# Pooled attention feeding a tanh-shrink MLP: the order of the first loads, and what follows from it

## Chip, cores and metric

The kernel runs on one core of a Trainium2 chip. The time is the device time of one execution in microseconds, as the median of several executions. A profiled execution gives a trace beside it: every instruction of each engine, every DMA, and the clock that was granted to TensorE.

## What is computed

```python
# q, k, v: (8 batches, 8 heads, 576 positions, 64); w_in (512, 2048); w_out (2048, 512)
k_p = k.reshape(B, H, 72, 8, D).mean(axis=3)        # keys and values pooled by 8
v_p = v.reshape(B, H, 72, 8, D).mean(axis=3)
attn = softmax(q @ k_p.T / sqrt(D))
x = (attn @ v_p).transpose(0, 2, 1, 3).reshape(4608, 512)
h = x @ w_in
out = (h - tanh(h)) @ w_out
```

## The kernel before

**Stages.** The 4608 tokens are treated in nine groups of 512 (`g` from 0 to 8): of each batch, the first 512 positions are a group, and the last 64 positions of all eight batches make the ninth. For a group, the hidden layer is computed in 16 tiles of 128 (`mlp_h` for group 0, `h_pair` later): TensorE multiplies by `w1b`, ScalarE takes tanh, VectorE subtracts into `Gt`. Then comes the output product with `w2b`. Group 0 does it plainly (`mlp_o(0, tb, qd, gts)`: token block `tb`, quarter `qd` of the hidden tiles, in the order 0, 8, 4, 12); later groups use a scheme of seven block products with sums of weights (`w2s`) and of tiles, which VectorE prepares (`w_sum`, called as `sum0` to `sum3`) while group 0's output is computed.

**Pooling and layout.** For each batch, 576 pooled rows (8 heads of 72) are loaded as four pairs of heads (144 rows each): 128 rows of each pair as tile `t` from 0 to 3 (`load_main`), and the 16 left-over rows of each pair together as tile `NM` = 4 (`load_dense`, 64 partitions of 2 KB, or `load_left` in four small loads). `pool_k` adds the eight positions in three VectorE steps (lines 268, 276, 281) into `kd`. TensorE turns `kd` by a matmul with the identity (`turn_tile`, L363), and VectorE copies the result into `KB` (`kb_main`, `kb_left`). q is cast (L891), turned on TensorE (`q_pe_transpose`, L228) and copied by ScalarE (L144). `scores_wide` multiplies q by KB (L409) and takes exp on ScalarE (L424). The v of batch 0 is pooled on TensorE (`v_pe_pool`, L900) out of `v_bf`, then masked by VectorE into `VB`. `av_pair` multiplies E by VB (L498) and divides (L954, L955); `x0_turn` turns x for the hidden layer.

**Order.** The whole order is written out by hand[...]. Loads are issued by three engines: SyncE (SP) for k of batch 0, ScalarE for q of batch 0 and for the left-over rows of k and v, GpSimd (POOL) for everything that is cast while it is loaded (v of batch 0, `w1b`, `w2b`, q of batch 1), and for v of batch 1. `after(load_k(1), w1_dmas[1])` makes SP hold back k of batch 1 until w1's second quarter has landed; `after(load_k(2), w2_dmas[2])` likewise holds back k of batch 2 until the third load of w2 has landed. `warm_pe` issues matmuls on zeros, of no use but to keep TensorE busy. [...]

Batch 1's attention runs in among group 0's MLP: `pool_k(1, nc.gpsimd, last=nc.vector)` has GpSimd do the first addition and VectorE the two others, with the reorder of q (`q1_reorder`, L256) between them; then `k_transpose`, `q_pe_transpose`, `scores_wide` stand between the `mlp_o` groups.

Of the kernel before, what the change touches and what calls it, by code (L numbers as in the profile page):

```python
# [8 lines left out]
FP32 = mybir.dt.float32  # L9
# [20 lines left out]
NT = 5  # L30
# [4 lines left out]
NM = 4  # L35
# [8 lines left out]
def kernel(  # L44
# [9 lines left out]
    nc = tc.nc  # L54
# [75 lines left out]
        .rearrange("p (h d) -> p h d", h=H)  # L130
    )
    q_raws = {}
    rot = [0]

    def ps_any(shape, dtype, name):
        pool, tag = [(ps_a, "ps_a"), (ps_h, "hT_ps")][rot[0] % 2]
        rot[0] += 1
        return pool.tile(shape, dtype, name=name, tag=tag)

    evac_n = [0]  # L140

# [7 lines left out]
    def load_main(src, dst, b, t0, t1, eng=nc.sync):  # L149
        return eng.dma_start(out=dst[:, t0:t1, :], in_=src[b, 0:128, t0:t1, :])  # L150
# [7 lines left out]
    def load_dense(src, dst, b, eng=nc.sync):  # L158
        return eng.dma_start(
            out=dst[0 : NM * LO, NM, :], in_=src[b, 128:PR, :, :]  # L160
        )

    def load_k(b, eng=nc.sync):
        return [
            load_main(k_pairs, k_raw[b % 2], b, 0, NM, eng),
            load_dense(k_pairs, k_raw[b % 2], b, eng),
        ]
# [86 lines left out]
    def q1_reorder():  # L254
        for h in (0, 4):
            nc.vector.tensor_copy(  # L256
                out=q_bf[:, 0:R, h : h + 4, :].rearrange("p j h d -> p h j d"),
                in_=q1_bf[:, h : h + 4, :, :],
            )

    def pool_k(b, eng, t0=0, t1=NT, last=None, dep=None):
        r = k_raw[b % 2].rearrange("p t (j d) -> p t j d", d=D)[:, t0:t1, :, :]
        if b not in kdups:
            kdups[b] = work.tile([128, NT, 2, D], BF16, name="kd", tag="kd", bufs=1)
        kd = kdups[b][:, t0:t1, :, :]
        n = t1 - t0
        for ta, tb in halves(n, b):
            first = eng.tensor_tensor(  # L268
                out=r[:, ta:tb, 0:4, :],
                in0=r[:, ta:tb, 0:4, :],  # L270
                in1=r[:, ta:tb, 4:8, :],
                op=ALU.add,
            )
            if dep is not None and ta == 0:
                after([first], dep)
        (last or eng).tensor_tensor(
            out=r[:, :, 0:2, :], in0=r[:, :, 0:2, :], in1=r[:, :, 2:4, :], op=ALU.add
        )
        if b == 1:
            q1_reorder()  # L280
        kd_done = (last or eng).tensor_tensor(
            out=kd,
            in0=r[:, :, 0:1, :].to_broadcast([128, n, 2, D]),
            in1=r[:, :, 1:2, :].to_broadcast([128, n, 2, D]),
            op=ALU.add,
        )
        return kd_done
# [68 lines left out]
    def kb_left(kb, ps, eng):  # L356
        eng(
            out=kb[D:128, :].rearrange("p (t x) -> p t x", x=KP)[:, :, 128 : 128 + LO],
            in_=ps[D:128, 0 : NM * LO].rearrange("p (x t) -> p t x", t=NM),
        )  # L360

    def turn_tile(dst, kd, t):
        nc.tensor.matmul(  # L363
            dst,
            lhsT=kd[:, t, :, :].rearrange("p a d -> p (a d)"),
            rhs=ident[:, :],
            start=True,
            stop=True,
        )
# [47 lines left out]
    def scores_wide(b, ts):  # L417
        if b not in E_tiles:
            E_tiles[b] = work.tile([128, H, S], BF16, name="E", tag="E", bufs=1)[:, 0:NT, :]
        E = E_tiles[b]  # L420
        for t in ts:
            ps = ps_any([128, QA], FP32, "s_ps")
            score_mms(b, t, ps[:, :], False)
            nc.scalar.activation(out=E[:, t, 0:QA], in_=ps[:, :], func=ACT.Exp, scale=SCALE)  # L424
# [350 lines left out]
        .rearrange("p (t n) -> p t n", t=NT)  # L775
    )
    zeros = xT_last[:, 3, :, :].rearrange("p f c -> p (f c)")
    w1_dmas = []
    w2_dmas = []

    def load_w1(c):
        w1_dmas.append(
            nc.gpsimd.dma_start(
                out=w1b[:, :, c * 512 : (c + 1) * 512], in_=w1_src[:, :, c * 512 : (c + 1) * 512]
            )
        )

    def load_w2(i, n):
        w2_dmas.append(
            nc.gpsimd.dma_start(out=w2b[:, i : i + n, :], in_=w2_src[:, i : i + n, :])  # L790
        )

    def after(lds, dep):
        for ld in lds:
            tc.add_manual_dep(
                ld.ins,
                dep.ins.name,
                mybir.DependencyInfo(mybir.DependencyClass.Sync, mybir.DependencyReason.DATA),
            )

    def warm_pe(n, cols=512, b0=4):
        for _ in range(n):
            nc.tensor.matmul(  # L803
                bank(b0, [128, cols]), lhsT=zeros[:, 0:128], rhs=zeros[:, 0:cols], start=True, stop=True
            )
# [3 lines left out]
    def load_q0(h0, h1):  # L809
        return nc.scalar.dma_start(  # L810
            out=t0[:, h0:h1, 0:R, :],
            in_=q[0, h0:h1, 0:QA, :].rearrange("h (p j) d -> p h j d", j=R),
        )
# [5 lines left out]
    load_q0(0, 2)  # L819
    load_main(k_pairs, k_raw[0], 0, 1, 2)  # L820
    load_q0(2, 4)
    load_main(k_pairs, k_raw[0], 0, 2, 4)
    load_q0(4, 8)
    load_dense(k_pairs, k_raw[0], 0, nc.scalar)
    load_dense(v_pairs, v_raw[1], 0, nc.scalar)

    warm_pe(9)
# [28 lines left out]
        out=spread.rearrange("p (t x) -> p t x", x=32)[:, :, 0:LO],  # L856
        in_=ident[:, 0 : NM * LO].rearrange("p (x t) -> p t x", t=NM),
    )
    for c in range(4):
        load_w1(c)  # L860
    load_w2(0, 4)
    nc.gpsimd.tensor_copy(out=v_bf[:, NM, :], in_=v_raw[1][:, NM, :])
    nc.gpsimd.dma_start(out=q1_tail[:QT], in_=q[1, :, QA:S, :].rearrange("h p d -> p h d"))
    nc.gpsimd.dma_start(
        out=q1_bf, in_=q[1, :, 0:QA, :].rearrange("h (p j) d -> p h j d", j=R)
    )
    load_w2(8, 4)
    nc.gpsimd.memset(w2s[64:128, 3, 6:8, :], 0.0)
    nc.gpsimd.memset(k_raw[1][:, NM, :], 0.0)
    nc.gpsimd.memset(v_raw[0][:, NM, :], 0.0)  # L870
    nc.gpsimd.memset(KB[1][:, :], 0.0)
    load_main(v_pairs, v_raw[1], 1, 0, 2, nc.gpsimd)
    load_w2(4, 4)

    after(load_k(1), w1_dmas[1])

    def k_turn(ta, tb):
        ps = ps_any([128, tb - ta, 128], FP32, "kT_ps")
        for t in range(ta, tb):
            turn_tile(ps[:, t - ta, :], kdups[0], t)  # L880
        kb_main(KB[0], ps, ta, tb, (nc.vector.tensor_copy, nc.vector.tensor_copy))

    def k_turn_left():
        ps = ps_any([128, 128], FP32, "kT_ps")
        turn_tile(ps[:, :], kdups[0], NM)
        kb_left(KB[0], ps, nc.vector.tensor_copy)

    pool_k(0, nc.vector, 0, 1)
    pool_k(0, nc.vector, 1, 2)
    def q_turn(eng, h0, h1):  # L890
        eng(  # L891
            out=q_bf[:, 0:R, h0:h1, :].rearrange("p j h d -> p h j d"),
            in_=t0[:, h0:h1, 0:R, :],
        )
# [26 lines left out]
    nc.scalar.dma_start(out=t0[:QT, :, R, :], in_=q[0, :, QA:S, :].rearrange("h p d -> p h d"))  # L921
    q_turn(nc.scalar.copy, 4, 6)
    q_turn(nc.scalar.copy, 6, 8)
    pool_k(0, nc.vector, 2, 4)
    warm_pe(6)
    k_turn(2, 4)
    pool_k(0, nc.vector, NM, NT)
    warm_pe(2)
    q_pe_transpose(0, (2, 3), "act")
    vs0 = v_pe_pool(0, 2, ident, 4)  # L930
    v_main(VB[0], vs0, nc.vector, 0, 2)
    warm_pe(1, b0=3)
    scores_wide(0, (2, 3))
    v_ps = v_pe_pool(NM, NT, spread)
    k_turn_left()
    v_left(VB[0], v_ps[:, 0, :, :], nc.vector)
    warm_pe(1, b0=3)
    scores_wide(0, (NM,))
    vs1 = v_pe_pool(2, 4, ident, 3)
    v_main(VB[0], vs1, nc.vector, 2, 4)  # L940
    load_left(v_pairs, v_raw[1], 1, nc.scalar)
    pool_v1(NM, NT, nc.gpsimd)
    v1_last = load_main(v_pairs, v_raw[1], 1, 2, 4, nc.gpsimd)
    load_w2(12, 4)
    gts = []

    def av_pair(p, half, b0, ns=(0, 1, 2)):
# [34 lines left out]
        pool = None if half or tp else bank(b0, [128, TG])  # L982
        mlp_h_mms(0, i, 2 * half, 2 * half + 2, pool, 2 * tp, 2 * tp + 2)

    av_pair(0, 0, 1, (0, 1))
    av_pair(1, 0, 6, (0, 1))
    av_pair(0, 0, 1, (2,))
    av_pair(1, 0, 6, (2,))
    av_pair(0, 1, 3)
    warm_pe(1, b0=5)  # L990
    x0_turn((0, 1), 0, 0, nc.scalar.copy)
# [21 lines left out]
    for i in range(5, NHID):  # L1013
        mlp_h(0, i, gts, bank(i % 5 if i > 5 else 5, [128, TG]))
        if i == 7:
            q_pe_tail(0)
        if i == 9:
            scores_tail(0)
        if i == 11:
            ps_a.n = 0  # L1020
            av(0, 4, ps_any, True)
    def turn1(blk):
        x_pe_transpose(1, blk, x_pairs[1, blk // 2][:, blk % 2])

# [15 lines left out]
    def sum3(k0):  # L1040
        return w_sum(w2s[:, 3, :, :], b21, b11, ALU.subtract, k0=k0, k1=k0 + 4)

    pool_k(1, nc.gpsimd, last=nc.vector)
    mlp_o(0, 0, 0, gts)
    mlp_o(0, 1, 0, gts)
    mlp_o(0, 2, 0, gts)
    mlp_o(0, 3, 0, gts)
    q_pe_transpose(1, (0, 1), "act")
    k_transpose(1, ps_any, (nc.vector.tensor_copy, nc.vector.tensor_copy))
    sum1(0)  # L1050
    mlp_o(0, 0, 1, gts)
    q_pe_transpose(1, (2, 3), "act")
    q_pe_tail(1)
    sum2(0)
    sum0(0)
    pool_v1(0, 2)
    scores_wide(1, (0, 1))
    mlp_o(0, 1, 1, gts)
    scores_wide(1, (2, 3))
    scores_ends(1)  # L1060
    negated(0)
# [1 line left out]
    pool_v1(2, 4)  # L1063
    sum1(4)
    sum0(4)
    mlp_o(0, 2, 1, gts)
    mlp_o(0, 3, 1, gts)
    mlp_o(0, 0, 2, gts)
    mlp_o(0, 1, 2, gts)
    mlp_o(0, 2, 2, gts)  # L1070
# [141 lines left out]
```

## Time and profile before

| | |
|---|---|
| median of 3 runs | 283.22 us (283.02 to 283.3) |
| profiled execution | 285.69 us, span 283.7 us |
| TensorE busy | 275.3 us, 97% of the span |
| VectorE, ScalarE, GpSimd busy | 221.2, 155.0, 116.1 us |
| mean granted TensorE clock | 0.991 |
| HBM read, written | 36.70 MB, 9.44 MB |

The span runs from the first to the last instruction of the profiled execution; its own time is 2.0 us longer. Busy time of an engine is what its instructions took, matmuls on zeros included. The chain that ended last, which the profile follows back from the last instruction, tells which waits count: only a wait in that chain lengthens the run. PE is TensorE, DVE VectorE, ACT ScalarE, POOL GpSimd, SP SyncE; L268 is line 268 of the kernel.

### The profile page before, as it was taken

What the parts mean: (1) busy time and instruction counts of PE and PEld (TensorE: products, weight loads), DVE (VectorE), ACT (ScalarE), POOL (GpSimd) and SP (SyncE); (2) the same over time, 40 slices, a digit from 0 to 9 for tenths busy, and PEclk for the clock granted to TensorE, in tenths of its full rate; (3) what the DMA queues carried; (4) which work ended last, traced back from release to release, by engine and by line L of the source; (5) the groups of instructions that cost most, each with busy time, mean ns of one, the idle gap of its engine ahead of it and who ended that gap; (6) DMA issues with size and microseconds to landing.
All of it is one profiled execution on the core that took longest, in us unless ns stands there. A gap on an engine that the chain in (4) does not pass through costs nothing.

```text
span 283.7 us, 5494 instructions
## 1 busy us (share of the span) xinstructions
PE 275.3 (97%) x2174; PEld 181.2 (64%) x2174; DVE 221.2 (78%) x336; ACT 155.0 (55%) x209; POOL 116.1 (41%) x131
## 2 busy tenths in 40 slices
PE   7799999999999999999999999999999999999993
PEld 3375455545885588458944895489547954884583
DVE  6567889689966997699859985999599849936983
ACT  4548654796528662766286718671867056216610
POOL 8655400894398029802990199009900200010000
PEclk9899999999999999999999999999999999999998
DMA  7999999988857895779578968896640440011014
GB/s 241 234 213 269 234 241 336 256 188 267 228 104 184 251 327 91 170 238 343 93 160 236 334 119 144 239 335 133 127 150 1 79 155 2 0 75 76 0 39 111
DMA packets 66491, 49.82 MB, mean 176 GB/s; under 512 B 42104, under 2 KB 55944, under 8 KB 66466
## 3 DMA queue, kind: packets, MB, share of 16 engines
q1 hardware_dynamic: 55538, 33.87, 47.1%
q0 software_dynamic: 8736, 13.77, 19.8%
q10 hardware_dynamic: 2192, 1.84, 2.2%
q8 instruction: 17, 0.28, 0.5%
q14 instruction: 8, 0.07, 0.1%
HBM read 36.70 MB, written 9.44 MB: 163 GB/s over the span
## 4 chain that ended last, share of the span: by engine, by line
PE 94%; DMA 3%; DVE 1%; SPq 0%; ACT 0%; issue 0%; DVEq 0%
PE PS L644 39%; PE PS L713 35%; PE PS L602 5%; PE PS L631 5%; PE PS L483 3%; DMA k_raw<-in_k_dram 3%; PE PS L457 3%; PE PS L498 1%; PE PS L409 1%; PE PS L900 1%; PE PS L803 1%; PE PS L580 0%; PE PS L228 0%; PE PS L967 0%; SPq L150 0%; DVE k_raw L268 0%
## 5 line engine op out<-in xcount | busy, mean ns | idle before, releaser
L644 PE MATMUL PS<-xT,w1b 128*128 128x512 bf16 (+1 forms) x504 | 98.0, 356 | 0.0
L670 DVE TENSOR_TENSOR Gt<-PS,TS 128x1024 bf16<-128x1024 f32 x56 | 68.3, 1222 | 33.6 <-ACT TS L669 33.6
L644 PEld LDWEIGHTS <-w1b 128*128 128x128 f16 x576 | 56.2, 98 | 53.0
L669 ACT ACTIVATE TS<-PS 128x1024 f32<-128x1024 f32 x56 | 57.3, 1024 | 29.7 <-PE PS L644 27.4
L757 POOL TENSOR_TENSOR m<-O,m 128x512 f32<-128x512 f32 x6 | 7.6, 1259 | 75.1 <-ACT m L755 53.5
L713 PE MATMUL PS<-w2s,Dg 128*128 128x256 f16 x256 | 30.2, 273 | 0.0
L268 POOL TENSOR_TENSOR k_raw<-k_raw 128x512 f32<-128x512 f32 (+2 forms) x13 | 21.1, 1634 | 20.1 <-DVE w2s L696 17.1
L478 ACT ACTIVATE E<-PS 72x1024 bf16<-72x1024 f32 (+1 forms) x30 | 26.0, 929 | 3.9 <-PE PS L457 3.7
L713 PEld LDWEIGHTS <-Gt 128*128 128x128 bf16 x256 | 23.5, 97 | 6.9 <-issue 2.4
L713 PEld LDWEIGHTS <-P 128*128 128x128 bf16 x256 | 24.5, 98 | 3.1
L713 PEld LDWEIGHTS <-Dg 128*128 128x128 bf16 x256 | 24.6, 97 | 2.9
L678 DVE TENSOR_TENSOR P<-Gt 128x1024 bf16<-128x1024 bf16 (+1 forms) x31 | 22.0, 708 | 0.5
L764 ACT COPY m<-PS 128x512 f32<-128x512 f32 x8 | 4.7, 586 | 29.6 <-PE PS L713 29.6
L729 POOL DMA_DIRECT2D out_dram<-O x14 | 7.7, 553 | 31.7 <-DVE O L767 29.5
L688 DVE TENSOR_TENSOR Dg<-Gt 128x1024 bf16<-128x1024 bf16 x32 | 20.4, 683 | 0.0
L534 DVE TENSOR_TENSOR x_sb<-PS,rden 128x512 bf16<-128x512 f32 x28 | 19.4, 692 | 1.0
L293 POOL TENSOR_TENSOR v_raw<-v_raw 128x512 f32<-128x512 f32 (+1 forms) x12 | 18.7, 1575 | 0.0
L713 PE MATMUL PS<-w2s,Gt 128*128 128x256 f16 x128 | 16.4, 273 | 0.0
L713 PE MATMUL PS<-w2b,P 128*128 128x256 f16 x128 | 16.3, 273 | 0.0
L713 PE MATMUL PS<-w2s,Q 128*128 128x256 f16 x128 | 16.3, 272 | 0.0
L713 PE MATMUL PS<-w2b,Gt 128*128 128x256 f16 x128 | 16.3, 272 | 0.0
L1174 ACT COPY O<-PS 128x512 f32<-128x512 f32 x7 | 4.1, 585 | 21.9 <-PE PS L713 21.9
(124 smaller groups left out, 399.4 us busy)
## 6 DMA issues: line engine op xcount, KB each, us to landing
k_raw<-in_k_dram SPq DMA_DIRECT2D x7, 1024.0 KB, 6.0
out_dram<-O POOLq DMA_DIRECT2D x14, 512.0 KB, 4.8
v_raw<-in_v_dram SPq DMA_DIRECT2D x6, 1024.0 KB, 8.6
q_raw<-in_q_dram SPq DMA_DIRECT2D x6, 1024.0 KB, 11.4
w1b<-in_moe_w_in_dram POOLq DMA_DIRECT2D x4, 512.0 KB, 13.8
w2b<-in_moe_w_out_dram POOLq DMA_DIRECT2D x4, 512.0 KB, 21.5
v_raw<-in_v_dram POOLq DMA_DIRECT2D x2, 512.0 KB, 18.8
out_dram<-O SPq DMA_DIRECT2D x2, 512.0 KB, 4.7
```

The source lines that it names most:

```text
L268: first = eng.tensor_tensor(out=r[:, ta:tb, 0:4, :], in0=r[:, ta:tb, 0:4, :], in1=r[:, ta:tb, 4:8, :], op=ALU.add,)
L293: eng.tensor_tensor(out=r[:, ta:tb, 0:4, :], in0=r[:, ta:tb, 0:4, :], in1=r[:, ta:tb, 4:8, :], op=ALU.add,)
L478: nc.scalar.activation(out=e, in_=ps, func=ACT.Exp, scale=SCALE)
L534: nc.vector.tensor_tensor(out=x_sb[:, :, :, :], in0=ps[:, :, :, 0:D], in1=rden[:, :, :, :].to_broadcast([128, 2, 4, D]), op=ALU.mult,)
L602: nc.tensor.matmul(h_tiles[i][:, t0 * 128 : t1 * 128], lhsT=w1b[:, fb, i * 128 : (i + 1) * 128], rhs=xT[g][:, t0:t1, fb, :], start=(fb == ...
L631: nc.tensor.matmul(o_ps[:, :], lhsT=gts[i][:, tb * 128 : (tb + 1) * 128], rhs=w2b[:, i, :], start=(i == 0), stop=(i == NHID - 1),)
L644: nc.tensor.matmul(dst[:, t0 * 128 : t1 * 128], lhsT=w1b[:, fb, i * 128 : (i + 1) * 128], rhs=x[:, t0:t1, fb, :], start=(fb == 0), stop=(f ...
L669: nc.scalar.activation(out=t2, in_=PS[:, b0 : b0 + 2, :], func=ACT.Tanh)
L670: nc.vector.tensor_sub(out=Gt[:, p, :, :], in0=PS[:, b0 : b0 + 2, :], in1=t2)
L678: nc.vector.tensor_tensor(out=P[:, a:b, :], in0=Gt[:, a:b, 0, :], in1=Gt[:, a:b, 1, :], op=ALU.add)
L688: return nc.vector.tensor_tensor(out=Dg[:, a:b, :, :], in0=Gt[:, a:b, :, 0:HT], in1=Gt[:, a:b, :, HT:TG], op=ALU.subtract,)
L713: nc.tensor.matmul(part(g, bk, tt), lhsT=lhs(k, slice(tt * 128, (tt + 1) * 128)), rhs=rhs[:, k, :], start=(first and k == 0 and (tt == 0 o ...
```

## The change

Loads. The left-over keys of batch 0 are loaded by SP ahead of tiles 2 and 3, no longer by ScalarE. w1's first quarter is loaded in two halves. k of batch 1 is loaded by GpSimd right after w1, without the wait on w1's second quarter. w2's second quarter to be used (tiles 8 to 11) is loaded ahead of q of batch 1. The left-over v of batch 1 is loaded by SP in place of ScalarE. The halves of v of batch 1 and the two last loads of w2 are issued later in the program, the last of each after GpSimd's part of `pool_k(1)`.

Head. The left-over keys are pooled before tiles 2 and 3, and the three tiles are turned as one group (`k_turn_rest`). The left-over v is pooled on TensorE right after the first half of v, a warm-up matmul is gone, the left-over scores come first, and the value groups are no longer split. The PSUM banks of the head are a written-out list.

Middle. GpSimd's and VectorE's part of `pool_k(1)` move up behind hidden tile 14; `k_transpose` moves ahead of the fourth `mlp_o` group; `q1_reorder` leaves `pool_k` and comes after `sum1(0)`; two `mlp_o` groups move up among the turning of q and the scores.

```diff
@@ pool_k
-        if b == 1:
-            q1_reorder()
@@ first loads
     load_main(k_pairs, k_raw[0], 0, 1, 2)
     load_q0(2, 4)
+    load_dense(k_pairs, k_raw[0], 0)
     load_main(k_pairs, k_raw[0], 0, 2, 4)
     load_q0(4, 8)
-    load_dense(k_pairs, k_raw[0], 0, nc.scalar)
     load_dense(v_pairs, v_raw[1], 0, nc.scalar)
@@ GpSimd's queue
-    for c in range(4):
-        load_w1(c)
+    for c0, c1 in ((0, 256), (256, 512), (512, 1024), (1024, 1536), (1536, 2048)):
+        load_w1(c0, c1)
+    load_main(k_pairs, k_raw[1], 1, 0, NM, nc.gpsimd)
+    nc.gpsimd.memset(k_raw[1][:, NM, :], 0.0)
+    nc.gpsimd.tensor_copy(out=v_bf[:, NM, :], in_=v_raw[1][:, NM, :])
+    load_dense(k_pairs, k_raw[1], 1, nc.gpsimd)
     load_w2(0, 4)
-    nc.gpsimd.tensor_copy(out=v_bf[:, NM, :], in_=v_raw[1][:, NM, :])
+    nc.gpsimd.memset(w2s[64:128, 3, 6:8, :], 0.0)
+    load_w2(8, 4)
     nc.gpsimd.dma_start(out=q1_tail[:QT], in_=q[1, :, QA:S, :].rearrange("h p d -> p h d"))
+    nc.gpsimd.memset(v_raw[0][:, NM, :], 0.0)
+    nc.gpsimd.memset(KB[1][:, :], 0.0)
     nc.gpsimd.dma_start(
         out=q1_bf, in_=q[1, :, 0:QA, :].rearrange("h (p j) d -> p h j d", j=R)
     )
-    load_w2(8, 4)
-    nc.gpsimd.memset(w2s[64:128, 3, 6:8, :], 0.0)
-    nc.gpsimd.memset(k_raw[1][:, NM, :], 0.0)
-    nc.gpsimd.memset(v_raw[0][:, NM, :], 0.0)
-    nc.gpsimd.memset(KB[1][:, :], 0.0)
-    load_main(v_pairs, v_raw[1], 1, 0, 2, nc.gpsimd)
-    load_w2(4, 4)
-
-    after(load_k(1), w1_dmas[1])
@@ new helpers
+    def k_turn_rest(b0):
+        ps = bank(b0, [128, 3, 128])
+        for t in range(2, NT):
+            turn_tile(ps[:, t - 2, :], kdups[0], t)
+        kb_main(KB[0], ps[:, 0:2, :], 2, 4, (nc.vector.tensor_copy, nc.vector.tensor_copy))
+        kb_left(KB[0], ps[:, 2, :], nc.vector.tensor_copy)
+
+    banks = iter((5, 0, 6, 1, 7, 2, 0, 6, 1, 0, 5))
+
+    def ps_any(shape, dtype, name):
+        return bank(next(banks), shape)
@@ head
+    pool_k(0, nc.vector, NM, NT)
     pool_k(0, nc.vector, 2, 4)
     warm_pe(6)
-    k_turn(2, 4)
-    pool_k(0, nc.vector, NM, NT)
+    k_turn_rest(5)
     warm_pe(2)
     q_pe_transpose(0, (2, 3), "act")
     vs0 = v_pe_pool(0, 2, ident, 4)
     v_main(VB[0], vs0, nc.vector, 0, 2)
-    warm_pe(1, b0=3)
-    scores_wide(0, (2, 3))
-    v_ps = v_pe_pool(NM, NT, spread)
-    k_turn_left()
+    v_ps = v_pe_pool(NM, NT, spread, 2)
     v_left(VB[0], v_ps[:, 0, :, :], nc.vector)
     warm_pe(1, b0=3)
-    scores_wide(0, (NM,))
+    scores_wide(0, (NM, 2, 3))
     vs1 = v_pe_pool(2, 4, ident, 3)
     v_main(VB[0], vs1, nc.vector, 2, 4)
-    load_left(v_pairs, v_raw[1], 1, nc.scalar)
+    ps_a.n = 7
+    load_left(v_pairs, v_raw[1], 1)
     pool_v1(NM, NT, nc.gpsimd)
-    v1_last = load_main(v_pairs, v_raw[1], 1, 2, 4, nc.gpsimd)
-    load_w2(12, 4)
+    load_main(v_pairs, v_raw[1], 1, 0, 2, nc.gpsimd)
+    load_w2(4, 4)
...
-    av_pair(0, 0, 1, (0, 1))
-    av_pair(1, 0, 6, (0, 1))
-    av_pair(0, 0, 1, (2,))
-    av_pair(1, 0, 6, (2,))
+    av_pair(0, 0, 1)
+    av_pair(1, 0, 6)
@@ hidden tiles of group 0, in the loop over i
+        if i == 14:
+            pool_k(1, nc.gpsimd, last=nc.vector)
+            load_main(v_pairs, v_raw[1], 1, 2, 4, nc.gpsimd)
+            load_w2(12, 4)
@@ output of group 0 and attention of batch 1
-    pool_k(1, nc.gpsimd, last=nc.vector)
     mlp_o(0, 0, 0, gts)
     mlp_o(0, 1, 0, gts)
     mlp_o(0, 2, 0, gts)
+    k_transpose(1, ps_any, (nc.vector.tensor_copy, nc.vector.tensor_copy))
     mlp_o(0, 3, 0, gts)
+    sum1(0)
+    q1_reorder()
+    mlp_o(0, 0, 1, gts)
+    mlp_o(0, 1, 1, gts)
     q_pe_transpose(1, (0, 1), "act")
-    k_transpose(1, ps_any, (nc.vector.tensor_copy, nc.vector.tensor_copy))
-    sum1(0)
-    mlp_o(0, 0, 1, gts)
     q_pe_transpose(1, (2, 3), "act")
     q_pe_tail(1)
     sum2(0)
     sum0(0)
     pool_v1(0, 2)
+    mlp_o(0, 2, 1, gts)
     scores_wide(1, (0, 1))
-    mlp_o(0, 1, 1, gts)
+    mlp_o(0, 3, 1, gts)
     scores_wide(1, (2, 3))
     scores_ends(1)
...
-    mlp_o(0, 2, 1, gts)
-    mlp_o(0, 3, 1, gts)
     mlp_o(0, 0, 2, gts)
```

More of the change, by code (lines that the diff above doesn't have):

```diff
@@ L132 @@
     q_raws = {}
[L133 to L138, printed above, removed]
     evac_n = [0]
@@ L777, with load_w1 @@
     zeros = xT_last[:, 3, :, :].rearrange("p f c -> p (f c)")
-    w1_dmas = []
     w2_dmas = []
[L781 to L786, printed above, removed]
+    def load_w1(c0, c1):
+        nc.gpsimd.dma_start(out=w1b[:, :, c0:c1], in_=w1_src[:, :, c0:c1])
     def load_w2(i, n):
@@ L881, in k_turn @@
         kb_main(KB[0], ps, ta, tb, (nc.vector.tensor_copy, nc.vector.tensor_copy))
[L883 to L886, printed above, removed]
+    def k_turn_rest(b0):
[7 more added lines that the diff above has]
+        return bank(next(banks), shape)
     pool_k(0, nc.vector, 0, 1)
```

## The prediction

> **What bounds the kernel now.** I read the page's chain of waits first: 94% of the span hangs on TensorE, so whatever TensorE does not wait for is free. From about 19 us on it hardly waits. What is left to win lies in the head, before the first MLP matmul, and at about 40 us.
>
> The chain in order of time (start us, us, what) shows the head:
>
> ```profile
> 1.74 7.66 DMA k_raw<-in_k_dram
> 9.41 0.02 issue
> 9.43 0.70 DVE k_raw L268
> 10.13 0.02 issue
> 10.16 0.44 DVE k_raw L276
> 10.60 0.02 issue
> 10.62 0.44 DVE kd L281
> 11.05 0.05 issue
> 11.10 0.28 PE PS L363 x2
> ```
>
> Everything hangs on one load, keys 2 to 4 of batch 0 (`load_main(..., 2, 4)`, 512 KB, SP's queue), usable at 9.41. I call that moment X. Three VectorE steps later (X+1.69) TensorE turns those keys. TensorE's warm-up matmuls ended at 9.14; it then idles 1.96 us. The answer by windows (us, length, busy us and instructions of PE, PEld, DVE, ACT, POOL, granted clock, DMA share, GB/s) shows the price of that pause and how full the DMA engines are:
>
> ```profile
> 5.00:6.00 1.00, 0.64 (x7) 0.25 (x5) 0.93 (x4) 0.98 (x3) 0.94 (x4) 1.00 0.77 279
> 6.00:7.00 1.00, 1.00 (x11) 0.57 (x9) 0.86 (x5) 1.00 (x3) 1.00 (x2) 1.00 1.06 375
> ...
> 12.00:13.00 1.00, 1.00 (x13) 0.90 (x11) 0.90 (x4) 0.92 (x2) 1.00 (x3) 0.56 1.21 196
> 13.00:14.00 1.00, 1.00 (x6) 0.44 (x4) 0.55 (x2) 0.15 (x1) 0.70 (x2) 0.50 1.23 198
> 14.00:15.00 1.00, 1.00 (x12) 0.63 (x10) 0.00 (x0) 0.85 (x2) 0.96 (x2) 0.50 1.21 194
> 15.00:16.00 1.00, 1.00 (x10) 0.32 (x9) 0.65 (x2) 0.32 (x2) 0.94 (x3) 0.73 1.26 203
> ```
>
> The clock is halved for 3.41 us, from 12.44 to 15.85 by the trace's clock record. A 512-column matmul costs 0.43 there, 0.22 outside.
>
> Further on in the chain, one wait is left in the stretch that the change reorders:
>
> ```profile
> 39.63 0.24 PE PS L228 x4
> 39.87 0.02 issue
> 39.89 0.59 ACT qT L144
> 40.48 0.04 issue
> 40.53 0.38 PE PS L409
> ```
>
> A score of batch 1 waits for a PSUM bank that ScalarE is still emptying. The 0.59 is not all lost: from 34.59 to 47.09 (12.50 us) the pieces of TensorE's work add up to 12.29, so about 0.2 us is idle.
>
> [...] earlier, after a load ends (3.2, 4.5 us), the same queue's next starts only about 0.5 us later, and the other queue runs alone. [...] engines finish keys 2 to 4 from 6.4 to 8.6 us[...]. [...]
>
> **The change, head.** (a) The left-over keys (64 rows of 2 KB, `load_dense`) move from ScalarE's queue to SP's, ahead of keys 2 to 4. That is 4 packets per engine: 4 x 84 ns = 0.34 us alone[...]. The issue (0.66 us on ScalarE) is paid on SP, which now issues keys 2 to 4 at about 2.4 instead of 1.74, still long before their packets start at 5.0. One more load may cost one more start gap, 0.5. From below, 0: SP's queue moved almost nothing from 4.5 to 5.0, and the rows may fit there. From above, 1.9: all 32 packets per engine of q heads 4 to 8, now issued first, run ahead (1.5 us) plus 0.34. I take 0.7, between 0.34 and 0.9.
>
> (b) The three VectorE steps for the left-over keys (0.42+0.29+0.29) move ahead of keys 2 to 4. VectorE idles 2.51 us before 9.43, so they are hidden if the rows land by about 8.3; behind keys 0 to 2, landed at 4.99, they should by 7.
>
> (c) TensorE's work from the first turn to the first attention-value matmul. Before, at full clock: turns 0.28, warm-up 0.43, q turns 0.45, v pooling 0.55 (that at 15.86), warm-up 0.22, two scores 0.43, left-over v 0.30 (an estimate from 0.42 at half clock), turn 0.07, warm-up 0.22, left-over score 0.22, v pooling 0.55: 3.72. Starting at 11.10, 1.34 is done by 12.44, the half-clock stretch does 3.41/1.9 = 1.79 (1.9 from 0.99 against 0.55 for v pooling and 0.43 against 0.22), the remaining 0.59 ends at 16.44; the trace has 16.41, so the model holds. After: one warm-up fewer, 3.50, ends at 16.2 with X unchanged: -0.22. Since the first value group then runs all six matmuls at once, its reciprocal (L954, 17.10 before) no longer waits for the second group's: end of v pooling plus six matmuls 0.36 plus 0.2 latency gives 16.73. So -0.37 with X unchanged, and each us of delay of X passes one to one[...]. At +0.7: **+0.33**.
>
> (d) ScalarE loses one issue (0.66) ahead of its table load, and later four for the left-over v of batch 1 (1.78 in all from 15.98). Its next work there is at 18.52: nothing.
>
> **The change, GpSimd's queue.** (e) w1's first quarter in two loads: one issue more (0.76). w1 is no bound: TensorE reaches it at 19.1 without a wait. (f) k of batch 1 leaves SP, where it waited 15.8 us for w1's second quarter, and follows w1 on GpSimd. Before GpSimd's copy of left-over v (at 11.53, after 1.96 of waiting) there now stand one more w1 issue 0.76, k's 0.74 and a memset 0.53, less w2's issue 0.78: it gets there at 10.8 instead of 9.57, still early. (g) GpSimd's 12th and 14th loads waited 1.8 and 0.8 us for its 4th and 6th to land, so I count eight in flight. w2's third load and the adding of k are now behind such a wait, for w1's last piece, about 25 us; k itself I put at 28.5 (30.66 before). GpSimd has idle time there. (h) w2's first quarter now lies behind k. By 31 us the queues had moved w1, k and that quarter before, too, so it lands then again; it is needed at 34.42. w2's next part moves ahead of q, q lands where that part did (36), needed at 39. The last parts keep their places. Cost zero while the queue stays full; if it runs dry by an issue that waits, up to 0.5.
>
> **The change, 34 to 47 us.** (i) Two VectorE steps for k of batch 1 (0.82 each) now stand before the last hidden tile's subtraction; that ends at 37.3 instead of 35.94. The fourth output matmul group needs its bank at 37.46. (j) The q reorder (0.76) comes after a weight sum and ends at 39.85; TensorE asks for it at 40.05. (k) An output group now stands between q's turns and the scores, which covers the bank wait: -0.2. Bounds -0.3 and +0.4, as (i) and (j) clear by only 0.2 each. I take **-0.2**.
>
> Sum: +0.33 - 0.2 = +0.13, say +0.2 with the thin margins. The profiled execution took 285.69 with a span of 283.7, 2.0 around it; the sum is against that span. The median, 283.22, is 2.5 below that execution, and I carry the difference over: 283.4.
>
> **Rivals.** *Hidden rows* (0.20): the rows use the gap at 4.5 to 5.0 and X stays within 0.2. Then -0.37 - 0.2 = -0.57, to -0.36: 282.65 to 282.9, and 282.4 if a second gap closes. For it: the low DMA share of 0.77 at 5 to 6 us. [...]
> *q goes first* (0.25), the slower side: SP's and ScalarE's loads have so far been served in turn, and the inserted load gives q heads 4 to 8 the turn of keys 2 to 4. X moves by up to 1.9: -0.57 + 1.9 = +1.3, 284.5. It decides once X is later than 10.55 (+1.14), where the sum passes +0.57. For it: the turn-taking up to 5 us[...].
> *A late VectorE* (0.10): (i) or (j) miss by more than they clear, and the output groups wait 0.5 to 1: 283.9 to 284.4. For it: VectorE is busy 24 of 28 us from 22 to 50.
> *Does it do what it says?* Left-over keys cannot be used first if they land after keys 2 to 4[...].
>
> **Numbers.** My forecast (X +0.3 to +1.1) has 0.45: 283.4, own range 282.9 to 283.8. About 0.2%, 0.57 us, is what a measurement of this kernel can tell from no change. Faster by more takes most of the first rival: 0.17. Slower by more: the second, most of the third and the upper edge of the forecast: 0.38. Within: 0.45. Range 282.5 to 284.7.
>
> **What would show it.** In the new profile: the chain's k_raw load ends near 10.1; L268 for it starts there with the left-over steps done before; three turns in one group; half clock still about 12.4 to 15.9; the first L954 near 17.4; no ScalarE step near 40 us in the chain. Wrong if X is at or below 9.5 or beyond 10.6, if the half-clock stretch moves or vanishes, or if waits for kd, q_bf or w2b appear on TensorE between 34 and 48 us.

## The result and the profile after

The changed kernel takes **286.0 us** (median of 4, 285.79 to 286.41) against 283.25 beside it: ratio 1.0101, 95% interval 1.0083 to 1.0118. It is slower by 2.75 us, far outside the range of the prediction (282.5 to 284.7). Its profiled execution took 286.41, with a span of 284.4 and a mean granted clock of 0.994.

The chain of waits of the kernel after, in order of time (start us, us, what; line 262 is now what 268 was, 270 was 276, 273 was 281, 355 was 363, 594 was 602):

```profile
2.50 8.30 DMA k_raw<-in_k_dram
...
10.83 0.70 DVE k_raw L262
...
11.55 0.72 DVE k_raw L270
...
12.30 0.43 DVE kd L273
...
12.78 0.47 PE PS L355 x3
```

Keys 2 to 4 are again what everything hangs on, but SP issues them at 2.50 and VectorE gets them at 10.83. The first w1 matmul (L594) starts at 20.53. The answer by windows of the same kernel (us, length, busy us and instructions of PE, PEld, DVE, ACT, POOL, granted clock, DMA share, GB/s):

```profile
5.00:6.00 1.00, 1.00 (x7) 0.54 (x6) 0.71 (x2) 0.18 (x2) 0.94 (x4) 1.00 1.02 294
...
12.00:13.00 1.00, 0.22 (x3) 0.22 (x4) 0.69 (x2) 0.00 (x0) 0.55 (x1) 0.93 1.31 185
13.00:14.00 1.00, 1.00 (x6) 0.45 (x4) 0.69 (x3) 0.00 (x0) 0.52 (x1) 0.50 1.34 183
14.00:15.00 1.00, 1.00 (x12) 1.00 (x11) 0.02 (x1) 0.43 (x1) 0.77 (x2) 0.50 1.42 190
15.00:16.00 1.00, 1.00 (x16) 1.00 (x14) 0.07 (x1) 0.64 (x2) 0.53 (x1) 0.50 1.39 203
```

The clock is halved from about 12.9 to 16.3. TensorE's waits over the whole run show no wait for `w1b`, `w2b` or `q_bf`; beside the start, only the wait for the keys is left, 3.4 us long:

```profile
PE PS L355 <- DVE kd L273: 3.6, 2, 3.4
PE PS L790 <- DVE xT_last L802: 1.3, 1, 1.3
```

Of the middle, the chain of the kernel after holds only TensorE's own work; the ScalarE step of before (L144) is gone from it:

```profile
38.66 2.62 PE PS L623 x12
41.28 0.89 PE PS L222 x16
...
42.17 0.28 PE PS L234 x4
42.45 0.86 PE PS L623 x4
```

**The base was not an ordinary execution.** One more profile of the kernel before (`before_again`, below) took 283.4, 2.3 less than the execution that the prediction was worked from. Its chain:

```profile
1.75 6.54 DMA k_raw<-in_k_dram
8.31 0.70 DVE k_raw L268
...
17.04 0.66 PE PS L602 x6
```

VectorE starts on the keys at 8.31, not 9.43, and the clock is full from 12 to 16 us. Why the recorded execution got them later, with the same order of issues, stays open. Of 98 executions of the kernel before that stood beside the experiments, one had a mean clock below 0.995 (0.991, 285.7 us). All four of the kernel after have 0.992 to 0.994.

**Where 2.9 us went** (spans 281.5 and 284.4; `before_again` against after, one execution each):

| | us |
|---|---|
| keys 2 to 4 later, 8.31 to 10.83 | +2.52 |
| three VectorE steps on them, 1.67 to 1.95 | +0.28 |
| half clock between the turn and the first w1 matmul | +1.56 |
| the new order of the head, at full clock | -0.87 |
| from the first w1 matmul to the first matmul of group 1 | -0.08 |
| behind the last VectorE instruction | -0.5 |
| sum | +2.9 |

The third and fourth rows come from the time between the first turn of keys 2 to 4 and the first w1 matmul: 9.98 to 17.04 (7.06) in `before_again`, 12.78 to 20.53 (7.75) in the kernel after, and 6.19 in three experiments that have the new order and full clock (`after_warm20`, `after_q_held`, `after_q_later`). The 0.87 belongs to a late turn: `before_rows_first`, with the old order, full clock and its turn at 12.51, takes 6.95, so 0.1 comes from the lateness; and `after_v_first`, with the new order and its turn at 10.46, takes 6.75, since TensorE there waits 0.5 for casts of q. The last row is the piece from L1180 (L1173 after) to the end of the span, 4.3 against 3.8. Each profile with the old queue of GpSimd has 4.1 to 4.3 there, each with the new one 3.7 to 4.0. Why, I have not found.

### The profile page after: what moved, and what is told of

It reads as the page before. It is cut to its first block, busy times and chain, and to the rows that moved or that the text cites. A ratio compares the mean times of both kernels' runs of the same rounds, so it can differ in the third digit from the quotient of the medians.

```text
span 284.4 us, 5492 instructions
## 1 busy us (share of the span) xinstructions
PE 275.6 (97%) x2173; PEld 182.1 (64%) x2173; DVE 221.5 (78%) x336; ACT 155.0 (54%) x209; POOL 118.6 (42%) x134
## 3 DMA queue, kind: packets, MB, share of 16 engines
q0 software_dynamic: 9584, 14.95, 21.1%
## 4 chain that ended last, share of the span: by engine, by line
PE 94%; DMA 3%; DVE 1%; issue 0%; SPq 0%
PE PS L636 39%; PE PS L705 35%; PE PS L594 5%; PE PS L623 5%; DMA k_raw<-in_k_dram 3%; PE PS L475 3%; PE PS L449 3%; PE PS L490 1%; PE PS L401 1%; PE PS L222 1%; PE PS L892 1%; PE PS L790 1%; PE PS L572 0%; PE PS L957 0%; PE PS L355 0%; DVE k_raw L270 0%
## 5 line engine op out<-in xcount | busy, mean ns | idle before, releaser
L262 POOL TENSOR_TENSOR k_raw<-k_raw 128x512 f32<-128x512 f32 (+2 forms) x13 | 21.1, 1634 | 21.2 <-DVE w2s L688 18.9
L705 PE MATMUL PS<-w2b,P 128*128 128x256 f16 x128 | 16.3, 273 | 0.0
L705 PE MATMUL PS<-w2b,Gt 128*128 128x256 f16 x128 | 16.3, 272 | 0.0
L705 PE MATMUL PS<-w2s,Q 128*128 128x256 f16 x128 | 16.3, 272 | 0.0
```

What stands on the lines that cost most here:

```text
L262: first = eng.tensor_tensor(out=r[:, ta:tb, 0:4, :], in0=r[:, ta:tb, 0:4, :], in1=r[:, ta:tb, 4:8, :], op=ALU.add,)
L705: nc.tensor.matmul(part(g, bk, tt), lhsT=lhs(k, slice(tt * 128, (tt + 1) * 128)), rhs=rhs[:, k, :], start=(first and k == 0 and (tt == 0 o ...
```

## The experiments

In each, the kernel before ran beside it, with medians of 283.2 to 283.3.

**1. The load order alone.** `before_rows_first`, the kernel before with the left-over keys issued by SP ahead of keys 2 to 4:

```diff
+    load_dense(k_pairs, k_raw[0], 0)
     load_main(k_pairs, k_raw[0], 0, 2, 4)
     load_q0(4, 8)
-    load_dense(k_pairs, k_raw[0], 0, nc.scalar)
```

> The kernel before with one edit: the left-over keys are loaded by SP ahead of keys 2 to 4, not by ScalarE. Theory A and theory B alike: X moves from 9.4 to about 10.8, and TensorE's pause grows to 3.3 us. Theory A adds the half clock in every execution: 1.4 + 1.3 to 1.7 slower, about 286. Theory B: 1.4 slower, about 284.6. If the delay of X comes from other parts of the change (GpSimd's queue): 283.3.

Measured: 286.5 us, ratio 1.0118 (1.0101 to 1.0135). Keys usable at 10.85, turns at 12.51 after 2.89 of waiting. This one load, moved from ScalarE to SP, costs 3.3 us. The rest of the change seems to give 0.5 back; the executions of the two kernels overlap (285.92 to 286.82 here, 285.79 to 286.41 after).

`after_head_undone` is the opposite: the kernel after with loads, order and PSUM banks of the head as before, and only GpSimd's queue, the middle and the load of the left-over v of batch 1 changed.

> The changed kernel with its head undone: the left-over keys on ScalarE's queue, the order of the head's matmuls and the banks as in the kernel before; GpSimd's new queue and the order from 34 to 47 us stay. If the whole slowdown lies in the head: no slower than before, and faster by the 0.2 that the middle was costed at, as w2's second quarter now lands in time: 282.9 to 283.2. If GpSimd's queue costs something: 283.6 or more.

Measured: 282.55, ratio 0.9978 (0.9966 to 0.9991). Keys usable at 7.8, first w1 matmul at 16.73. So the loss lies in what this kernel undoes, the head and its loads, and the rest of the change is a small gain.

**2. An ordinary execution of the kernel before.** `before_again` has no edit.

> The kernel before, profiled once more. Its recorded profile took 285.69 us, 2.4 above its timed executions. Theory A (that execution was not typical): about 283.2, X near 8.3 and no half clock in the head. Theory B (the profile costs the difference): 285.5 or more, X at 9.4 and half clock from about 12.5.

Measured: 283.4; its lines are shown above. TensorE waits 0.81 for the keys and keeps its full clock.

**3. Is it a turn that the inserted load takes?** My first theory was that the queues of SP and ScalarE are served load by load in turn, so that an inserted load on SP gives q heads 4 to 8 the turn of keys 2 to 4. `before_small_load` inserts 32 KB:

```diff
     load_q0(2, 4)
+    nc.sync.dma_start(out=k_raw[1][0:16, 0, :], in_=k_pairs[1, 0:16, 0, :])
     load_main(k_pairs, k_raw[0], 0, 2, 4)
```

> The kernel before with one small load of 32 KB (16 rows of k of batch 1, one packet for each DMA engine, to a place that is loaded again later) put into SP's queue ahead of keys 2 to 4; nothing else changed. Turn theory (SP's and ScalarE's loads are served in turn, and an inserted load of any size gives q heads 4 to 8 the turn of keys 2 to 4): X later by about 2 us, at 10.3, and some 2.5 us slower, near 286. Bytes theory (the inserted bytes cost their own packets): X later by 0.1 to 0.3, at 8.5, 283.5.

Measured: 285.35, ratio 1.0087 (1.0068 to 1.0107). Keys usable at 9.54, 1.2 later: less than the 2.5 of the kernel after. The time is not the keys' alone: ScalarE's last load was issued at 4.65 instead of 3.07, its table load followed at 5.25 instead of 3.70, and TensorE waited 1.9 for the first cast of q.

`after_v_first` moves one load of ScalarE ahead of another in the kernel after:

```diff
-    load_q0(4, 8)
     load_dense(v_pairs, v_raw[1], 0, nc.scalar)
+    load_q0(4, 8)
```

> The changed kernel with one edit: ScalarE issues the left-over v (128 KB) ahead of q heads 4 to 8, so that the left-over keys on SP are paired with a small load and not with the large one. Turn theory: X back from 10.8 to about 8.8 to 9.2, no half clock, 1.5 to 2.5 faster than the changed kernel: 283.5 to 284.5. Bytes theory (X is late by the left-over keys' own bytes and by more loads on the queue): X stays near 10.5, 286 within 0.4.

Measured: 282.94, ratio 1.0004 (0.9986 to 1.0022): the loss is gone. VectorE works on the keys from 8.80; TensorE waits 0.85. Turns explain it, but the swap also issues q heads 4 to 8 at 3.00, behind the keys (2.51). Two more kernels separate the count of loads from their time. `after_keys_merged` makes SP's first two loads one, so that keys 2 to 4 are the third load of SP, as q heads 4 to 8 are of ScalarE:

```diff
-    load_main(k_pairs, k_raw[0], 0, 0, 1)
+    load_main(k_pairs, k_raw[0], 0, 0, 2)
     load_q0(0, 2)
-    load_main(k_pairs, k_raw[0], 0, 1, 2)
```

> The kernel after, with its first two key loads (tile 0 and tile 1 of batch 0, 256 KB each) made into one load of 512 KB; SP still loads the same bytes in the same order, but left-over keys are now its second load and keys 2 to 4 its third. Theory (SP's and ScalarE's loads are served load by load in turn): keys 2 to 4 get their old place ahead of q heads 4 to 8, are usable at 8.3 to 9.0 instead of 10.8, VectorE's step L262 starts there, no half clock, and the time is 282.5 to 283.7, even though the first keys come later. Rival (the 128 KB of left-over keys ahead on the queue, or the order of bytes, delays keys 2 to 4): they stay at 10.5 to 11 and the time at 285.5 to 286.5.

Measured: 285.36, ratio 1.0081 (1.0068 to 1.0095); the keys come at 11.13. **The theory of turns falls.** SP still issued them at 2.51: the left-over keys ahead of them go into a tile that VectorE clears first (L803, 1.27 to 1.75), and their issue started at 1.78 here as in the kernel after. `after_left_behind` puts the left-over keys behind keys 2 to 4 on SP, and pools them behind:

```diff
-    load_dense(k_pairs, k_raw[0], 0)
     load_main(k_pairs, k_raw[0], 0, 2, 4)
+    load_dense(k_pairs, k_raw[0], 0)
```

> The kernel after, with the left-over keys still on SP but behind keys 2 to 4, and pooled behind them. Theory (turns): keys 2 to 4 are SP's third load again and usable at 8.3 to 8.6; q heads 4 to 8 keep their place too; the left-over keys land by about 10 and their three steps end near 11.1, when the three tiles are turned; no half clock; 282.5 to 283.5. Rival (any 128 KB more on SP's queue costs this much, or the turning of three tiles at once does): 284.5 to 286.

Measured: 282.71, ratio 0.9995 (0.9976 to 1.0014). Keys usable at 7.57. So neither more bytes on SP's queue nor the turning of three tiles shows a cost; the place ahead of keys 2 to 4 does.

**4. Is it the time of issue?** Left was this: of two loads on two queues, the one issued first is served first. Before, SP issued keys 2 to 4 at 1.74 and ScalarE q heads 4 to 8 at 1.8. Issuing the left-over rows costs SP 0.68, and the keys' issue moves to 2.50, behind q's.

`after_q_later` was meant to delay q's issue by moving ScalarE's table load ahead of it:

```diff
+    nc.vector.memset(warm[:, :], 0.0)
...
+    nc.scalar.activation(out=warm[:, :], in_=warm[:, :], func=ACT.Exp)
     load_q0(4, 8)
...
-    nc.vector.memset(warm[:, :], 0.0)
-    nc.scalar.activation(out=warm[:, :], in_=warm[:, :], func=ACT.Exp)
```

> The kernel after with ScalarE's first exp (with its table load, 1.3 us) moved ahead of its issue of q heads 4 to 8: the number and the order of loads on both queues stay as in the kernel after, but that issue starts at about 3.3 us instead of 1.8, behind SP's issue of keys 2 to 4 (2.5). Theory A (of two loads on two queues, the one that is issued first is served first): keys 2 to 4 are usable at 8.3 to 9.2, no half clock in most executions, 282.4 to 283.6. Theory B (the queues are served load by load, third against third; the inserted load takes the turn): q heads 4 to 8 still go first, keys 2 to 4 come at 10.5 to 11, 285 to 286.5.

Measured: 285.91, ratio 1.0109 (1.0092 to 1.0126), keys at 10.43. It decides nothing, as the timeline of ScalarE shows (start us, us, engine, line, what):

```profile
1.84 1.28 ACT L812 ACT_TABLE_LOAD   x1 [1.84 <-issue]
1.91 0.42 ACTq L797 DMA_DIRECT2D q_raw<-in_q_dram  x1
```

The issue ran beside the table load, at 1.91 and not at 3.3. So I moved the issue by a real wait. `after_q_held` holds q back in the kernel after, without touching number or order of the loads (ScalarE's issue of the left-over v and its table load, which follow, move along to 3.54 and 4.22):

```diff
+    nc.vector.memset(KB[0][:, :], 0.0)
+    kb_again = nc.vector.memset(KB[0][:, :], 0.0)
...
-    load_q0(4, 8)
+    after([load_q0(4, 8)], kb_again)
...
-    nc.vector.memset(KB[0][:, :], 0.0)
```

> The kernel after with ScalarE's issue of q heads 4 to 8 held back by a wait on a VectorE memset that ends at about 3.0 us (the memset of KB, done twice). The number and the order of loads on both queues stay those of the kernel after; only this issue moves from 1.8 to about 3.1, behind SP's issue of keys 2 to 4 at 2.5. Theory A (what is issued first is served first): keys 2 to 4 are usable at 8.3 to 9.2, q heads 4 to 8 land at 10 to 11, 282.5 to 283.7 in executions without half clock. Theory B (served load by load, third against third): keys 2 to 4 stay at 10.4 to 11 and the time at 285 to 286.5.

Measured: **282.31**, ratio 0.9963 (0.9949 to 0.9977), the fastest kernel of all and a little below what I had written; no execution of its eight had a clock below 0.998. First the operations on the q tile (line, engine, operation, count, issue time in ns as least/median/most, first and last start in us), then VectorE's timeline (start us, us, line, operation), then the answer by windows with the columns as above:

```profile
L797 ACTq DMA_DIRECT2D q_raw<-in_q_dram x3: 375/472/478, 0.8 to 3.1; - x3
```

```profile
8.94 0.69 DVE L262 TENSOR_TENSOR k_raw<-k_raw 128x512 f32<-128x512 f32 x1
9.66 0.42 DVE L270 TENSOR_TENSOR k_raw<-k_raw 128x256 f32<-128x256 f32 x1
```

```profile
13.00:16.00 3.00, 2.85 (x38) 1.87 (x35) 1.94 (x5) 1.91 (x4) 1.88 (x4) 1.00 1.31 206
```

q heads 4 to 8 are issued at 3.1, VectorE takes the keys at 8.94 without a wait, TensorE's only wait after the start is 0.9 for the first cast of q, and the clock stays full.

`before_keys_held` does the reverse to the kernel before: SP's issue of keys 2 to 4 waits for the memset of KB, with no load added or reordered.

```diff
+    kb_zero = nc.vector.memset(KB[0][:, :], 0.0)
...
-    load_main(k_pairs, k_raw[0], 0, 2, 4)
+    after([load_main(k_pairs, k_raw[0], 0, 2, 4)], kb_zero)
...
-    nc.vector.memset(KB[0][:, :], 0.0)
```

> The kernel before with SP's issue of keys 2 to 4 held back by a wait on the memset of KB (about 2.6 us instead of 1.74); no load is added, removed or reordered. Theory A (issue time): q heads 4 to 8, issued at 1.8, go first; keys 2 to 4 are usable at 9.8 to 10.5, 0.9 less than in the kernel after since no left-over keys lie ahead; 284.5 to 286. Theory B (third against third, or the 128 KB ahead): keys 2 to 4 keep their place, usable at 8.3 to 8.8, and the time at 283.0 to 283.6.

Measured: 286.69, ratio 1.0120 (1.0107 to 1.0133), above the upper end of what I had written. Its chain:

```profile
2.66 7.76 DMA k_raw<-in_k_dram
10.44 0.70 DVE k_raw L268
```

**A delay of 0.9 us in the issue becomes 2.1 us in the arrival** (8.31 in `before_again`), with no load added or reordered. The 2.1 compares two single executions, and against the recorded one of the kernel before it is 1.0; the median is 3.4 longer than that of the kernel beside it. All profiles in one table:

| kernel | keys 2-4 issued | q 4-8 issued | VectorE takes the keys | median |
|---|---|---|---|---|
| after_left_behind | 1.7 | 1.8 | 7.57 | 282.71 |
| after_head_undone | 1.7 | 1.8 | 7.77 | 282.55 |
| before_queue | 1.7 | 1.8 | 7.81 | 284.4 |
| before_again | 1.7 | 1.8 | 8.31 | 283.4 (one) |
| before_warm14 | 1.7 | 1.8 | 8.33 | 284.27 |
| before_middle | 1.7 | 1.8 | 8.36 | 283.33 |
| after_v_first | 2.5 | 3.0 | 8.80 | 282.94 |
| after_q_held | 2.5 | 3.1 | 8.94 | 282.31 |
| before, as recorded | 1.7 | 1.8 | 9.43 | 285.69 (one) |
| before_small_load | 2.2 | 1.8 | 9.54 | 285.35 |
| after_q_later | 2.5 | 1.9 | 10.43 | 285.91 |
| before_keys_held | 2.7 | 1.8 | 10.44 | 286.69 |
| after_warm20 | 2.5 | 1.8 | 10.80 | 285.13 |
| after | 2.5 | 1.8 | 10.83 | 286.0 |
| before_rows_first | 2.5 | 1.8 | 10.85 | 286.5 |
| after_keys_merged | 2.5 | 1.9 | 11.13 | 285.36 |

Where the keys are issued first they are taken by 8.94, with one exception: the recorded execution of the kernel before, at 9.43. Where they are issued second, they are not taken before 9.54. So the order of issue is not all that moves the arrival, but the two kernels that only hold back one issue move it both ways: 8.94 against 10.83, and 10.44 against 8.31. (In `after_v_first` and `after_q_held` VectorE was busy with the left-over keys until then; keys 2 to 4 had landed at 8.7 and 8.1.)

**5. What the half clock adds.** `after_warm20` is the kernel after with more matmuls on zeros ahead of the turns, so that TensorE waits less:

```diff
-    warm_pe(6)
+    warm_pe(20)
```

> The changed kernel with 20 warm-up matmuls in place of 6 ahead of the turn of keys 2 to 4, which fills TensorE's pause of 3.4 us (9.4 to 12.8). Theory A (half clock: the pause is now long enough to halve TensorE's clock in every execution, while most executions of the kernel before escape it): no half clock in the head, some 1.5 to 1.8 us faster than the changed kernel, about 284.3. Theory B (late keys alone: X is 1.4 us later, the clock costs both kernels the same): 286.0 unchanged within 0.3, or a little slower if the last warm-up matmul is late.

Measured: 285.13, ratio 1.0067 (1.0052 to 1.0082), 0.87 below the kernel after. The wait for the keys falls from 3.38 to 0.73, and no execution of four has a clock below 0.998. It gives back less than the 1.56 of the table: the turns come at 13.10, 0.32 later, since the first VectorE step took 1.33 instead of 0.70 here. `before_warm14` does the same to the kernel before, with 14:

> The kernel before with 14 warm-up matmuls in place of 6, which fills its pause of 1.96 us. Theory A: its timed executions mostly run at full clock in the head already, so 283.2 within 0.3, and the half clock of the profiled execution does not appear. Theory B (its head is halved in every execution, as in the profiled one): some 1.5 us faster, about 281.7.

Measured: 284.27, ratio 1.0034 (1.0021 to 1.0047). There the extra matmuls end behind the keys and hold up the turns until 11.16: there was no half clock to be saved. The time lies outside what I had written for either theory.

**6. Middle and queue.** `before_middle` is the kernel before with only the order between 34 and 47 us changed (`pool_k(1)` behind hidden tile 14, `k_transpose` and two `mlp_o` groups earlier, `q1_reorder` behind `sum1(0)`):

> The kernel before with the part of the change between 34 and 47 us alone (adding of k of batch 1 behind hidden tile 14, its turn ahead of the fourth output group, q reorder after the first weight sum, two output groups moved up). Prediction: 0.2 faster, 283.0. Rival (VectorE late): 0.3 or more slower.

Measured: 283.33, ratio 1.0004 (0.9996 to 1.0013). Its chain shows why nothing is gained:

```profile
13.07 23.26 DMA w2b<-in_moe_w_out_dram
...
36.37 1.89 PE PS L629 x8
```

With the groups moved up, TensorE waits for w2's second quarter until 36.33, which the full change loads ahead of q of batch 1. `before_queue` is the other half alone, GpSimd's queue as in the kernel after, the order of the middle as before:

> The kernel before with only the change of GpSimd's queue (w1's first quarter in two loads, k of batch 1 on GpSimd behind w1, w2's second quarter ahead of q of batch 1, the later loads moved along); head and the order between 34 and 47 us as before. It is the version with the head undone, less the middle. If the gain of that version (0.7, 282.55) lies in the queue: 282.4 to 282.7. If it lies in the middle together with the earlier second quarter of w2: 283.0 to 283.5, and the bank wait near 40 us (L228, ScalarE's copy L144, score L409) stays in the chain of waits.

Measured: 284.4, ratio 1.0044 (1.0031 to 1.0057), outside both of the ranges I gave. Its chain:

```profile
18.93 17.08 DMA w2s<-in_q_dram
...
36.03 0.76 DVE q_bf L257 x2
36.80 0.74 DVE kd L282
...
37.59 0.45 PE PS L364 x5
```

q of batch 1 now lands at 36.03, and `q1_reorder`, still inside `pool_k`, makes the keys of batch 1 wait for it. Neither half is of use alone; together (`after_head_undone`) they give 0.7, of which the reading of steps (i) to (k) below says where it arises.

## Why the prediction was wrong

**Step (a) failed, and with it the forecast.** I wrote that SP "now issues keys 2 to 4 at about 2.4 instead of 1.74, still long before their packets start at 5.0", and let that cost nothing. The issue moved as I said, to 2.50, and its place among the issues, with the half clock that came with the longer wait, was the whole loss. I priced bytes and start gaps on the queue, 0.7 us with 1.9 as the upper bound; measured was 2.5 against an ordinary execution, 1.4 against the recorded one. `after_keys_merged`, `after_q_held` and `before_keys_held` show that neither bytes nor order within the queue decide. That the left-over rows ran first did hold: VectorE worked on them from 7.77 to 8.85, ahead of the keys.

**The rival "q goes first" is what happened**, though not by turns: `after_keys_merged`, with keys 2 to 4 as SP's third load, takes them at 11.13. The rival's own formula comes out near: -0.57 + (10.80 - 9.41) = +0.82 on the recorded 285.69 gives 286.5, and the profiled execution after took 286.41. That is partly luck. Between these two profiles the turn-to-w1 stretch shrank by 0.47 and the stretch up to group 1 by 0.08, near -0.57 in sum though split otherwise; two terms that the formula lacks, +0.28 on VectorE and -0.5 at the end, largely cancel. It stood at 284.5 only because the sum was set on the median, 2.5 below.

**Carrying over the 2.5 us failed.** I took the gap between the profiled execution and the median for a constant. It was an execution with keys late by 1.1 and a half clock of its own: its first w1 matmul came at 19.32, in `before_again` at 17.04. All four executions of the kernel after have a mean clock that fits a half-clock stretch, and its profile has late keys, so its median lies near its profile, and the 2.5 must not be taken off. A gap of 2.5 us between the profile and a median whose three runs span 0.28 was a sign to be read.

**Step (c), half right.** The stretch itself was misread: the recorded execution has half clock from 12.13 to 15.54, as the mean of 0.56 from 12 to 13 says, not from 12.44 to 15.85. Its length is the same, so the sum that ends at 16.44 stands. I held the half-clock stretch to be common to both kernels and to lie at the same time in both, which was an estimate. The ordinary execution of before has none; after has one, 3.4 us long, from 12.85 to 16.27, worth 1.56. The gain of the new order was there and larger than I said: 0.87 between turn and first w1 matmul, with the late turn, against my 0.37 up to the first division.

**Not foreseen:** L270 took 0.72 instead of 0.43, while GpSimd's copy of left-over v ran from 11.12 to 11.98 beside it: 0.28 us.

**Steps (b), (d) to (h) held.** The left-over steps were hidden, ScalarE's missing issues bought nothing, and no wait for w1, w2 or q of batch 1 stands on TensorE. That (h) costs nothing holds only with the moved `q1_reorder`: `before_queue` pays 1.2 in the median without it, and 1.9 in the stretch from the first w1 matmul to group 1 (36.83 against 34.96).

**Steps (i) to (k): the sign was right, the size was not.** VectorE's thin margins held, so *A late VectorE* did not happen, and the bank wait left the chain. But the stretch shrank by 0.08 (34.96 to 34.88 us from the first w1 matmul to the first of group 1), not 0.2. In the median, queue and middle together gave 0.7. In the profiles of `after_head_undone` and `before_again`, 0.4 of it is the shorter end behind the last VectorE instruction and 0.3 an earlier first w1 matmul (16.73 against 17.04); no step of mine had either. The second comes with earlier keys: both profiles with the old head and the new queue take them at 7.8, the ordinary ones with the old queue at 8.3 to 8.4.

**What step (a) held for a bound is what the queues show.** Its price per piece was measured: in the recorded execution, from 5.6 to 8 us, SP's queue moved 199 packets and ScalarE's 448, with medians of 84 ns for 2 KB and 46 ns for 1 KB. In what order the pieces of two queues follow each other on one DMA engine no run here shows, and the 0.7 between 0.34 and 0.9 was my estimate; all of q heads 4 to 8 running ahead was my bound, 1.9. The queues from 5 to 6 us, with loads outstanding on both (q1 is SP's, q10 ScalarE's; packets, MB, share of 16 engines), in `before_again`, after, `after_q_held` and `before_keys_held`:

```profile
q1 hardware_dynamic: 116, 0.24, 69.3%
q10 hardware_dynamic: 82, 0.07, 21.1%
...
q10 hardware_dynamic: 300, 0.29, 101.5%
q1 hardware_dynamic: 1, 0.00, 0.5%
...
q1 hardware_dynamic: 129, 0.24, 91.0%
q10 hardware_dynamic: 49, 0.04, 11.3%
...
q10 hardware_dynamic: 375, 0.37, 107.3%
```

In the last, SP's queue moved nothing. One queue did most of the work, 69.3 to 107.3% against 0 to 21.1%, and which one followed the order of issue. What makes it so stays open.

## What to carry to other kernels

Before inserting a DMA ahead of an urgent one, write down the issue times of all loads that compete with it, over all queues: here the 0.68 us that one more issue takes lost the race to another queue, and 0.9 us of issue became 1 to 2 us of arrival; holding back the rival load won it again. A profile that lies further from the median than the runs lie from each other may not be what the median measures; look in it for what is unusual (a half clock, a late load) before any sum is made on it. When a wait of TensorE grows, price the clock with it: here a wait of 3.4 us came with a half clock worth 1.56 us.

## What was not expected of the hardware

- **Issue order across queues.** Of two loads of SP and ScalarE issued within 1 us of each other, at about 2 us, the one issued first got most of the bytes when both began to move, 3 us later: from 5 to 6 us its queue moved 0.24 to 0.37 MB and the other 0 to 0.07. In `before_keys_held` SP's queue moved nothing in that time; in the kernel after both queues shared the engines from 6 to 8 us (49.1% SP's, 55.2% ScalarE's). Shown for this pair of loads at the start of this kernel.
- **Half clock follows the wait, not always.** A mean clock of at most 0.994 fits one half-clock stretch of 3.4 us, by my estimate from the span: half of 3.4 is 0.6% of 284.4. With 2.7 to 3.4 us of waiting for the keys in the profile (`before_keys_held`, `before_rows_first`, `after_q_later`, after) 15 of 17 executions had it; with 1.9 (`after_keys_merged`) 1 of 6; with 0.7 to 0.9 (`after_left_behind`, `after_v_first`, `after_warm20`, `before_middle`, before) 8 of 147; without a wait for the keys (`after_q_held`, `after_head_undone`, `before_queue`, `before_warm14`) 2 of 39. The recorded execution of before, with 1.96, had it too. The waits are those of one profile for each kernel. The stretch lasts 3.41 us in the recorded execution of before (12.13 to 15.54) and 3.41 in that of after (12.85 to 16.27), with waits of 1.96 and 3.38; the profiled execution of `after_q_later` waited 3.12 and had a mean clock of 1.0. What sets the length, and why an execution with a long wait can go without, stays open.
- **An issue of ScalarE did not wait for its table load** in `after_q_later`: it started at 1.91 beside a table load of 1.28 us from 1.84.
- **A ninth load waited.** In `before_small_load` the ninth load on the two queues was issued at 4.65, 1.6 later than as the eighth in the kernel before. What released it stays open.
- **The end of the span**, behind the last VectorE instruction, is about 0.5 us shorter with the new queue of GpSimd, and keys 2 to 4 come about 0.5 us earlier with it when the head is the old one. Both causes stay open.
